# Adding a rank-1 term through ScalarE in PSUM instead of bf16 matmuls, splitting seven Strassen products into two groups, and loading the start-up differently

## Chip, cores, metric

One core of a Trainium2 chip. The metric is device time in microseconds, the median of several executions. All executions quoted here were in the fast state, with a granted TensorE clock of 0.988 to 0.996 (the single run of e4_constant_scale has state unknown and is used for durations only). The time of the kernel before was 2109.68 us (2107.85 to 2117.36, 3 runs).

## The reference

```python
def reference(x, w_in, w_out):            # x [8, 3008, 256], w_in [256, 2048], w_out [2048, 256], fp32
    X = np.fft.fft(np.fft.fft(x, axis=1), axis=2).real     # a 2-D Fourier transform, real part
    X = X.reshape(8 * 3008, 256)
    h = X @ w_in
    g = h * np.cos(h)
    return g @ w_out
```

The kernel uses symmetry. It transforms along the sequence only; the transform along the channels is folded into the first weight matrix. Position k and position -k of the sequence then share their work: with P the even part and Q the odd part, one hidden value is P+Q and its mirror is P-Q. One channel (channel 0) does not fit into the 128 rows of the even matmul and must be added by itself as a rank-1 term: its row over the positions, times its column of weights.

## The kernel before: the parts that matter

The main loop has 376 steps. A step fills one PSUM bank called hp with 512 columns: two blocks of 128 hidden units, side by side, each for 256 positions. Eight steps make a tile (256 positions and their mirrors). The second weight matrix is applied in Strassen's way: seven products of half-size blocks, with sums before and after, instead of eight. In each step the engines do the following. (A limb is one of the three bf16 numbers whose sum stands for one fp32 number.)

```python
def mlp1_even(T, s):                  # TensorE, into the PSUM bank hp
    hp = ppool.tile([128, 512], FP, tag="hp", bufs=2, name="hp")
    for i in range(2):                # P without channel 0, fp32
        matmul(hp[:, i*TW:(i+1)*TW], lhsT=Wc[:, f*128:(f+1)*128], rhs=Rr[:, pos:pos+TW], start=(i == 0), ...)
    for i in range(2):                # channel 0: nine bf16 rows (3 limbs x 3 limbs) stand for one fp32 row
        matmul(hp[:, i*TW:(i+1)*TW], lhsT=Wl[:, f*128:(f+1)*128], rhs=Rl[:, pos:pos+TW], start=False, ...)

def copy_even(T, s):  ...             # ScalarE: pt = -2 * hp            (-2P; TensorE must not go on before)
def mlp1_odd(T, s):   ...             # TensorE: hp += Ws' Ir            (now P+Q)
def copy_plus(T, s):  ...             # ScalarE: h[:, 0:512] = hp
def minus(T, s):      ...             # VectorE: h[:, 512:1024] = pt + hp, reversed   (the subtraction)
# h * cos(h): ScalarE rounds, VectorE takes the remainder, ScalarE sine, VectorE product

def sums(T, s):
    A[5] = A[3] + A[2]; A[4] = A[0] + A[5]              # VectorE
    d = spool.tile([128, 512], FP, tag="d", bufs=DB)
    nc.scalar.copy(out=d, in_=T.h[s][:, 0:512])         # ScalarE
    nc.gpsimd.dma_start(out=d, in_=T.h[s][:, 768:1280], accum_op=ALU.add)   # d += h, by DMA

def mlp2(T, s, between):              # seven Strassen products into four banks, 4 steps behind
    parts = (("Ma",0,B11,A[0]), ("Mb",0,B21,A[1]), ("Mb",1,T2,A[4]), ("Mc",0,T1,A[5]), ("Md",1,T4,A[2]),
             ("Mc",1,T3,d[:,0:256]), ("Md",0,B22,d[:,256:512]))   # mlp1_odd runs ahead of the last two
# ... at the end of a tile: combine(T), four VectorE adds in a row, after the next step's mlp1_even ...
```

The input of each batch but the first is folded (summed and subtracted with its mirror, which shrinks the transform) by 18 VectorE operations, one a step, in steps 10 to 27 of the 47 steps of the batch ahead of it. Four transforms of six fp32 matmuls each follow.

Of the kernel before, what the change touches and what calls it, by code (L numbers as in the profile page):

```python
# [12 lines left out]
BF = mybir.dt.bfloat16  # L13
# [6 lines left out]
ND = 256  # L20
# [9 lines left out]
LAG = 4  # L30
HB = 5
DB = 3
# [47 lines left out]
def _limb_consts():  # L80

    p = np.arange(128)
    i, j = p // 3, p % 3
    return -np.stack([i >= 1, i >= 2, j >= 1, j >= 2], axis=1).astype(np.float32)


@with_exitstack
def kernel(
# [16 lines left out]
    LC_dr = nc.inline_tensor(_limb_consts(), name="limb_masks")  # L105
# [27 lines left out]
    LC = cpool.tile([128, 4], FP, tag="LC")  # L133
    nc.scalar.dma_start(out=LC, in_=LC_dr.ap())

# [53 lines left out]
    w2r = w2.rearrange("p (q e a j) -> p q e a j", e=2, a=4, j=32)  # L189
    wor = moe_w_out.rearrange("(q p) (a e j) -> p q e a j", p=128, e=2, j=32)  # L190
    for e in range(2):
        for a in range(4):
            nc.sync.dma_start(out=w2r[:, :, e, a], in_=wor[:, :, e, a])
# [12 lines left out]

    Rl = cpool.tile([128, RING], BF, tag="Rl")
    Wl = cpool.tile([128, NDFF], BF, tag="Wl")
    nc.vector.memset(Wl, 0.0)
    nc.vector.memset(Rl, 0.0)  # L210
# [7 lines left out]
    r128_dr = dpool.tile([3, NB, HALF], BF, tag="r128", name="r128")  # L218
    wl_dr = dpool.tile([3, NDFF], BF, tag="wl", name="wl")
# [9 lines left out]
    def fold_weights():  # L229
        for q in range(NDFF // 512):  # L230
# [24 lines left out]
            if q % 2:  # L255
                load_row(q // 2)
        with nc.allow_non_contiguous_dma(reason="one row to columns"):
            nc.gpsimd.dma_start(
                out=wex, in_=wx_dr.rearrange("o (f p) -> p (o f)", p=128)
            )  # L260

    def load_row(half):
        cols = slice(half * 1024, (half + 1) * 1024)
        nc.gpsimd.dma_start(out=wx_dr[:, cols], in_=Ws[127:128, cols])
        wf = spool.tile([8, 128], FP, tag="wf", bufs=2, name="wf")
        nc.gpsimd.dma_start(
            out=wf, in_=wx_dr[0, cols].rearrange("(f p) -> f p", p=128)
        )
        state["wf", half] = wf

    def row_to_limbs(half):

        cols = slice(half * 1024, (half + 1) * 1024)
        l3 = spool.tile([8, 3, 128], BF, tag="l3", bufs=2, name="l3")
        split_limbs(state["wf", half], [l3[:, j] for j in range(3)])
        nc.gpsimd.dma_start(
            out=wl_dr[:, cols].rearrange("j (f p) -> f j p", p=128), in_=l3
        )
        for i in range(3):
            nc.gpsimd.dma_start(out=Wl[3 * i : 3 * i + 3, cols], in_=wl_dr[:, cols])  # L280

    def split_limbs(x, limbs):

        for n, limb in enumerate(limbs):
            pin(nc.vector.tensor_copy(out=limb, in_=x))
            if n < 2:
                pin(
                    nc.vector.tensor_tensor(out=x, in0=x, in1=limb, op=ALU.subtract)
                )

    def row_limbs(x, limb, out_, c):

        n = x.shape[0]
        for step in range(3):
            o = out_ if step == 2 else limb
            pin(nc.vector.tensor_copy(out=o, in_=x))
            if step < 2:
                pin(
                    nc.vector.scalar_tensor_tensor(
                        out=x,  # L300
                        in0=limb,
                        scalar=LC[0:n, c + step : c + step + 1],
                        in1=x,
                        op0=ALU.mult,
                        op1=ALU.add,
                    )
                )
# [766 lines left out]
```

## Time and profile before

| | busy, share of the span |
|---|---|
| TensorE (PE) | 97% |
| VectorE (DVE) | 84% |
| ScalarE (ACT) | 68% |
| span of the profiled run | 2105.9 us |

The head of the profile page of the kernel before, and its chain of waits (the work that ended last, followed back from the end):

```profile
span 2105.9 us, 26765 instructions
PE 2050.6 (97%) x9540; PEld 1703.0 (81%) x9540; DVE 1778.3 (84%) x2438; ACT 1428.1 (68%) x1976; POOL 352.3 (17%) x409
...
PE 83%; DVE 11%; DMA 2%; issue 2%; ACT 1%; another core or an unknown queue 1%; SPq 0%; DVEq 0%; POOL 0%; ACTq 0%
```

The chain is TensorE for 83% of the span. The busy share alone would not have told this: the skill's page "Trainium Kernel Development and Optimization" (Performance Expectations) warns that, because matmuls are pipelined, matmul busy time is a bad measure of how close a kernel is to the roofline. What can be read exactly is when matmuls start. One step in TensorE's timeline (start in us, duration, engine, line, operation, tiles; "x4" means four instructions, because the profile records each fp32 matmul twice):

```profile
1001.22 1.03 PE L633 MATMUL hp<-Rr,Wc 128*128 128x256 f32 x4
1002.08 0.38 PE L645 MATMUL hp<-Rl,Wl 128*128 128x256 bf16 x2
1002.30 0.60 PE L767 MATMUL Ma<-h,w_88 128*128 128x256 f32 x2
1002.73 0.59 PE L767 MATMUL Mb<-h,w_88 128*128 128x256 f32 x2
...
1004.03 0.59 PE L767 MATMUL Md<-h,T_119 128*128 128x256 f32 x2
1004.46 1.03 PE L670 MATMUL hp<-Ir,Ws 127*128 127x256 f32 x4
1005.32 0.60 PE L767 MATMUL Mc<-d,T_118 128*128 128x256 f32 x2
1005.76 0.59 PE L767 MATMUL Md<-d,w_88 128*128 128x256 f32 x2
1006.19 0.59 PE L633 MATMUL hp<-Rr,Wc 128*128 128x256 f32 x2
```

The step is 1006.19 - 1001.22 = 4.97 us. The fp32 products stand 0.43 us apart; the two limb matmuls take 1002.30 - 1002.08 = 0.22 us. No idle time is marked: TensorE's stream has no holes here.

The costs of the operations that the change touches, in the groups of instructions of the kernel before (columns: line, engine, operation, tiles, shapes, count | busy us in all, mean ns of one | idle time just before them and its releaser):

```profile
L659 ACT ACTIVATE pt<-hp 128x512 f32<-128x512 f32 x376 | 221.7, 590 | 227.0 <-PE hp L645 223.8
L706 ACT COPY d<-h 128x512 f32<-128x512 f32 x376 | 229.6, 611 | 68.7 <-DVE h L735 67.1
```

And what TensorE waited for between 36 and 160 us, the start-up (columns: us in total, times, longest):

```profile
PE hp L670 <- ACT pt L659: 20.4, 8, 11.7
PE hp L645 <- DMA Wl<-wl: 9.6, 1, 9.6
PE hp L633 <- DVE Rr L406: 2.5, 1, 2.5
```

The 11.7 us wait ends a chain that begins with a 10.8 us wait of VectorE for the single channel's DMA, so the start-up is held by loads twice.

### The profile page before, as it was taken

The page shows a single profiled execution, that of the slowest core. Times are in us where ns is not written, and L with a number is a line of the kernel's source. Part 1 is how long each engine was busy: PE and PEld are TensorE (multiplying, and loading weights), DVE is VectorE, ACT ScalarE, POOL GpSimd, SP SyncE. Part 2 cuts the span into 40 slices and gives each one's busy share as a digit, 9 for nine tenths or more (in the row PEclk, how much of TensorE's full clock was granted, in tenths as well). Part 3 has the DMA queues.
Part 4 walks back from the last instruction along what each step waited for, and adds up shares of the span by engine and source line. Part 5 has one row for each costly group of instructions (what it writes and reads, how often), then busy time and mean ns, then how long its engine had stood idle before and what let it go on. Part 6 is the DMA issues. An engine that isn't in the chain of part 4 may idle for free.

```text
span 2105.9 us, 26765 instructions
## 1 busy us (share of the span) xinstructions
PE 2050.6 (97%) x9540; PEld 1703.0 (81%) x9540; DVE 1778.3 (84%) x2438; ACT 1428.1 (68%) x1976; POOL 352.3 (17%) x409
## 2 busy tenths in 40 slices
PE   7779999999999999999999999999999999999998
PEld 3558888888888888888888878888788888888877
DVE  6489788997889878898789987899788997888867
ACT  2457667776677667776677766777677776777755
POOL 1111111121111111111111111111111111111111
PEclk9989999999999999999999999999999999999999
DMA  9933343343333333334333334333433332333323
GB/s 249 62 61 64 86 88 71 64 90 71 75 74 64 87 84 71 66 61 88 85 74 61 60 88 94 66 64 64 99 81 64 58 74 50 63 64 71 65 51 66
DMA packets 210510, 159.80 MB, mean 76 GB/s; under 512 B 156845, under 2 KB 156886, under 8 KB 209864
## 3 DMA queue, kind: packets, MB, share of 16 engines
q0 software_dynamic: 56880, 111.25, 28.6%
q1 hardware_dynamic: 153352, 46.84, 10.4%
q8 instruction: 75, 1.23, 0.3%
q14 instruction: 59, 0.48, 0.1%
q10 hardware_dynamic: 144, 0.00, 0.0%
HBM read 34.67 MB, written 24.78 MB: 28 GB/s over the span
## 4 chain that ended last, share of the span: by engine, by line
PE 83%; DVE 11%; DMA 2%; issue 2%; ACT 1%; another core or an unknown queue 1%; SPq 0%; DVEq 0%; POOL 0%; ACTq 0%
PE hp L670 14%; PE hp L633 13%; PE Mc L767 13%; PE Md L767 13%; PE Mb L767 13%; PE Ma L767 7%; PE hp L645 3%; PE da L391 3%; PE db L391 3%; DVE h L735 2%; DVE r L721 2%; DVE h L688 1%; DVE X L796 1%; DVE h L703 1%; ACT r L728 1%
## 5 line engine op out<-in xcount | busy, mean ns | idle before, releaser
L707 POOL DMA_DIRECT2D d<-h x376 | 323.8, 861 | 1662.4 <-ACT h L684 419.1
L721 DVE TENSOR_TENSOR r<-h,r 128x1024 f32<-128x1024 f32 x376 | 458.2, 1219 | 91.0 <-ACT r L713 91.0
L728 ACT ACTIVATE r<-r,halfpi 128x1024 f32<-128x1024 f32 x376 | 432.8, 1151 | 137.2 <-DVE r L721 136.5
L735 DVE SCALAR_TENSOR_TENSOR h<-h,r 128x1024 f32<-128x1024 f32 x376 | 458.2, 1219 | 72.8 <-ACT r L728 72.8
L670 PE MATMUL hp<-Ir,Ws 127*128 127x256 f32 x1504 | 393.4, 383 | 24.8 <-ACT pt L659 24.5
L713 ACT ACTIVATE r<-h 128x1024 int32<-128x1024 f32 x376 | 394.8, 1050 | 4.8 <-DVE h L688 3.7
L633 PE MATMUL hp<-Rr,Wc 128*128 128x256 f32 x1504 | 388.9, 381 | 2.5 <-DVE Rr L406 2.5
L659 ACT ACTIVATE pt<-hp 128x512 f32<-128x512 f32 x376 | 221.7, 590 | 227.0 <-PE hp L645 223.8
L684 ACT COPY h<-hp 128x512 f32<-128x512 f32 x376 | 219.9, 585 | 194.5 <-PE hp L670 194.2
L670 PEld LDWEIGHTS hp<-Ir,Ws 127*128 127x128 f32 x1504 | 278.8, 190 | 79.2 <-ACT pt L659 43.3
L688 DVE TENSOR_TENSOR h<-pt,hp 128x512 f32<-128x512 f32 x376 | 257.2, 684 | 88.2 <-ACT h L684 84.9
L633 PEld LDWEIGHTS hp<-Rr,Wc 128*128 128x128 f32 x1504 | 286.6, 191 | 49.0 <-DVE Rr L406 3.1
L706 ACT COPY d<-h 128x512 f32<-128x512 f32 x376 | 229.6, 611 | 68.7 <-DVE h L735 67.1
L767 PE MATMUL Ma<-h,w_88 128*128 128x256 f32 x752 | 225.6, 382 | 0.3 <-ACT X L781 0.3
L767 PE MATMUL Mc<-d,T_118 128*128 128x256 f32 x752 | 225.4, 381 | 0.4 <-DMA d<-h 0.4
L767 PE MATMUL Mb<-h,w_88 128*128 128x256 f32 x752 | 224.7, 380 | 1.0 <-DVE X L796 1.0
L767 PE MATMUL Mc<-h,T_116 128*128 128x256 f32 x752 | 224.4, 380 | 0.4 <-DVE X L796 0.4
L767 PE MATMUL Mb<-h,T_117 128*128 128x256 f32 x752 | 224.6, 380 | 0.0
L767 PE MATMUL Md<-h,T_119 128*128 128x256 f32 x752 | 224.2, 380 | 0.1
L767 PE MATMUL Md<-d,w_88 128*128 128x256 f32 x752 | 224.1, 380 | 0.0
L704 DVE TENSOR_TENSOR h<-h 128x256 f32<-128x256 f32 x376 | 159.8, 425 | 12.9
L703 DVE TENSOR_TENSOR h<-h 128x256 f32<-128x256 f32 x376 | 159.7, 425 | 12.9
(349 smaller groups left out, 1896.2 us busy)
## 6 DMA issues: line engine op xcount, KB each, us to landing
d<-h POOLq DMA_DIRECT2D x376, 256.0 KB, 3.2
out_dram<-tr SPq DMA_DIRECT2D x252, 64.0 KB
h<-in_moe_w_in_dram SPq DMA_DIRECT2D x4, 512.0 KB
w_88<-in_moe_w_out_dram SPq DMA_DIRECT2D x8, 256.0 KB
out_dram<-tr SPq DMA_DIRECT2D x128, 4.0 KB
out_dram<-tr SPq DMA_DIRECT2D x32, 56.0 KB
out_dram<-tr SPq DMA_DIRECT2D x32, 48.0 KB
out_dram<-tr SPq DMA_DIRECT2D x32, 40.0 KB
```

What stands on the lines that cost most here:

```text
L633: nc.tensor.matmul(hp[:, i * TW : (i + 1) * TW], lhsT=Wc[:, f * 128 : (f + 1) * 128], rhs=Rr[:, pos : pos + TW], start=(i == 0), stop=Fals ...
L659: nc.scalar.activation(out=T.pt[s], in_=T.hp[s], func=AF.Copy, bias=0.0, scale=-2.0)
L670: nc.tensor.matmul(T.hp[s][:, i * TW : (i + 1) * TW], lhsT=Ws[0:127, f * 128 : (f + 1) * 128], rhs=Ir[:, pos : pos + TW], start=False, sto ...
L684: pin(nc.scalar.copy(out=T.h[s][:, 0:512], in_=T.hp[s]))
L688: nc.vector.tensor_tensor(out=T.h[s][:, 1023:511:-1], in0=T.pt.pop(s), in1=T.hp.pop(s), op=ALU.add,)
L706: pin(nc.scalar.copy(out=d, in_=T.h[s][:, 0:512]))
L707: pin(nc.gpsimd.dma_start(out=d, in_=T.h[s][:, 768:1280], accum_op=ALU.add))
L713: nc.scalar.activation(out=r[:, 0:n].bitcast(I32), in_=h[:, 0:n], func=AF.Copy, bias=0.25, scale=1.0)
L721: nc.vector.tensor_tensor(out=r[:, 0:n], in0=h[:, 0:n], in1=k, op=ALU.subtract)
L728: nc.scalar.activation(out=r[:, 0:n], in_=r[:, 0:n], func=AF.Sin, bias=halfpi, scale=TWO_PI)
L735: nc.vector.scalar_tensor_tensor(out=h[:, 0:n], in0=h[:, 0:n], scalar=TWO_PI, in1=r[:, 0:n], op0=ALU.mult, op1=ALU.mult,)
L767: nc.tensor.matmul(T.M[bank][:, half * TW : (half + 1) * TW], lhsT=lhsT[:, s], rhs=rhs, start=(s == 0 and n in (0, 1, 3, 4)), stop=(s == 7 ...
```

## The change

The intent is to take the limb matmuls off TensorE. ScalarE writes channel 0 as a product (a row spread over all partitions, times a per-partition scale) into the hp bank, and the even and odd matmuls accumulate on top of it. That this can work at all is in the skill's page "PSUM — Partial Sum Buffer" (The four PSUM rules): ScalarE writes neither set nor clear the hidden written bits, and a matmul without the first-of-group flag adds where the bit is set. Here the start-up's weight-folding matmuls have set those bits in both hp banks and nothing clears them later. To make room on ScalarE the copy into d goes: the seven products are split into a group of three (3 steps behind), after which the DMA may add into h itself, and a group of four (4 steps behind). The end of a tile is split the same way.

```diff
+    def channel_0(T, s):
+        T.hp[s] = ppool.tile([128, 512], FP, tag="hp", bufs=2, name="hp")
+        for i in range(2):
+            nc.scalar.mul(T.hp[s][:, i*TW:(i+1)*TW], Rb[:, pos:pos+TW], wex[:, f:f+1])
 def mlp1_even(T, s):
-        hp = ppool.tile([128, 512], FP, tag="hp", bufs=2, name="hp")
-                    ... start=(i == 0) ...
+                    ... start=False ...
-        for i in range(2):                      # limb matmuls
-            nc.tensor.matmul(hp..., lhsT=Wl[...], rhs=Rl[...], ...)
 def sums(T, s):
-        d = spool.tile([128, 512], FP, tag="d", bufs=DB, name="d")
-        pin(nc.scalar.copy(out=d, in_=T.h[s][:, 0:512]))
-        pin(nc.gpsimd.dma_start(out=d, in_=T.h[s][:, 768:1280], accum_op=ALU.add))
-    def mlp2(...), def combine(T)
+    def products_1(T, s):   # Ma B11 A0; Mb B21 A1; Mb T2 A4; then
+        nc.gpsimd.dma_start(out=h[:, 0:512], in_=h[:, 768:1280], accum_op=ALU.add)
+    def products_2(T, s):   # Mc T1 A5; Md T4 A2; Mc T3 h[0:256]; Md B22 h[256:512]
+    def combine_1(T): ...   # Ma, Mb: one ScalarE copy, one VectorE add
+    def combine_2(T): ...   # Mc, Md: three VectorE adds
 # the loop
+        stage(i + 1, channel_0)                 # right after the rounding
+        stage(i - LAG1, products_1)             # LAG1 = 3
+        if ...: combine_1(...)
+        stage(i, mlp1_odd)
+        stage(i - LAG2, products_2)             # LAG2 = 4
+        stage(i, copy_plus)
+        if ...: combine_2(T)
 # start-up
-    eight loads of w_out in 128-byte pieces straight into w2
+    three loads in 1 KB rows, put into place by six ScalarE copies
-    limb arithmetic of the channel's row and weights;  at(2, load_ext)
+    load_ext() ahead of the loop
     (some other start-up operations move by one or two steps)
```

More of the change, by code (lines that the diff above doesn't have):

```diff
@@ L12 @@
 I32 = mybir.dt.int32
-BF = mybir.dt.bfloat16
 U32 = mybir.dt.uint32
@@ L29 @@
 BW = 3 * NE
-LAG = 4
+LAG1 = 3
+LAG2 = 4
 HB = 5
-DB = 3
 def _dft_consts():
@@ L77, in _row_consts @@
     return np.stack([neg, HALF - 5 - 6 * p, last], axis=1).astype(np.uint32)
-def _limb_consts():
-    p = np.arange(128)
-    i, j = p // 3, p % 3
-    return -np.stack([i >= 1, i >= 2, j >= 1, j >= 2], axis=1).astype(np.float32)
 @with_exitstack
@@ L104 @@
     IX_dr = nc.inline_tensor(_row_consts(), name="row_table")
-    LC_dr = nc.inline_tensor(_limb_consts(), name="limb_masks")
     cpool = ctx.enter_context(tc.tile_pool(name="consts", bufs=1))
@@ L132 @@
     nc.sync.dma_start(out=ix, in_=IX_dr.ap())
-    LC = cpool.tile([128, 4], FP, tag="LC")
-    nc.scalar.dma_start(out=LC, in_=LC_dr.ap())
     def load_x(b):
@@ L187, with place_w2 @@
             MC[ri, kodd] = m
-    w2r = w2.rearrange("p (q e a j) -> p q e a j", e=2, a=4, j=32)
-    wor = moe_w_out.rearrange("(q p) (a e j) -> p q e a j", p=128, e=2, j=32)
-    for e in range(2):
-        for a in range(4):
-            nc.sync.dma_start(out=w2r[:, :, e, a], in_=wor[:, :, e, a])
+    W2_PARTS = ((0, 6), (6, 12), (12, 16))
+    w2_parts = []
+    for f0, f1 in W2_PARTS:
+        st = spool.tile([128, 1536], FP, tag="h", bufs=HB, name="st")
+        nc.sync.dma_start(
+            out=st[:, 0 : (f1 - f0) * ND].rearrange("p (q c) -> p q c", c=ND),
+            in_=moe_w_out[f0 * 128 : f1 * 128, :].rearrange("(q p) c -> p q c", p=128),
+        )
+        w2_parts.append(st)
+    def place_w2(n):
+        f0, f1 = W2_PARTS[n]
+        src = w2_parts[n][:, 0 : (f1 - f0) * ND].rearrange(
+            "p (q a e j) -> p q a e j", a=4, e=2, j=32
+        )
+        dst = w2[:, f0 * ND : f1 * ND].rearrange(
+            "p (q e a j) -> p q e a j", e=2, a=4, j=32
+        )
+        for e in range(2):
+            pin(nc.scalar.copy(out=dst[:, :, e], in_=src[:, :, :, e]))
     halfpi = cpool.tile([128, 1], FP, tag="halfpi")
@@ L205 @@
     Ir = cpool.tile([127, RING], FP, tag="Ir")
-    Rl = cpool.tile([128, RING], BF, tag="Rl")
-    Wl = cpool.tile([128, NDFF], BF, tag="Wl")
-    nc.vector.memset(Wl, 0.0)
-    nc.vector.memset(Rl, 0.0)
+    Rb = cpool.tile([128, RING], FP, tag="Rb")
     T1 = cpool.tile([128, NF // 2, 128], FP, tag="T1")
@@ L217 @@
     Rb4 = cpool.tile([128, NB], FP, tag="Rb4")
-    r128_dr = dpool.tile([3, NB, HALF], BF, tag="r128", name="r128")
-    wl_dr = dpool.tile([3, NDFF], BF, tag="wl", name="wl")
+    r128_dr = dpool.tile([NB, HALF], FP, tag="r128", name="r128")
     wx_dr = dpool.tile([1, NDFF], FP, tag="wx", name="wx")
@@ L255, in fold_weights @@
             if q % 2:
-                load_row(q // 2)
-        with nc.allow_non_contiguous_dma(reason="one row to columns"):
-            nc.gpsimd.dma_start(
-                out=wex, in_=wx_dr.rearrange("o (f p) -> p (o f)", p=128)
-            )
-    def load_row(half):
-        cols = slice(half * 1024, (half + 1) * 1024)
-        nc.gpsimd.dma_start(out=wx_dr[:, cols], in_=Ws[127:128, cols])
-        wf = spool.tile([8, 128], FP, tag="wf", bufs=2, name="wf")
-        nc.gpsimd.dma_start(
-            out=wf, in_=wx_dr[0, cols].rearrange("(f p) -> f p", p=128)
-        )
-        state["wf", half] = wf
-    def row_to_limbs(half):
-        cols = slice(half * 1024, (half + 1) * 1024)
-        l3 = spool.tile([8, 3, 128], BF, tag="l3", bufs=2, name="l3")
-        split_limbs(state["wf", half], [l3[:, j] for j in range(3)])
-        nc.gpsimd.dma_start(
-            out=wl_dr[:, cols].rearrange("j (f p) -> f j p", p=128), in_=l3
-        )
-        for i in range(3):
-            nc.gpsimd.dma_start(out=Wl[3 * i : 3 * i + 3, cols], in_=wl_dr[:, cols])
-    def split_limbs(x, limbs):
-        for n, limb in enumerate(limbs):
-            pin(nc.vector.tensor_copy(out=limb, in_=x))
-            if n < 2:
-                pin(
-                    nc.vector.tensor_tensor(out=x, in0=x, in1=limb, op=ALU.subtract)
-                )
-    def row_limbs(x, limb, out_, c):
-        n = x.shape[0]
-        for step in range(3):
-            o = out_ if step == 2 else limb
-            pin(nc.vector.tensor_copy(out=o, in_=x))
-            if step < 2:
-                pin(
-                    nc.vector.scalar_tensor_tensor(
-                        out=x,
-                        in0=limb,
-                        scalar=LC[0:n, c + step : c + step + 1],
-                        in1=x,
-                        op0=ALU.mult,
-                        op1=ALU.add,
+                cols = slice((q - 1) * 512, (q + 1) * 512)
+                nc.gpsimd.dma_start(out=wx_dr[:, cols], in_=Ws[127:128, cols])
+                with nc.allow_non_contiguous_dma(reason="one row to columns"):
+                    nc.gpsimd.dma_start(
+                        out=wex[:, (q - 1) * 4 : (q + 1) * 4],
+                        in_=wx_dr[:, cols].rearrange("o (f p) -> p (o f)", p=128),
                     )
-                )
     def fold_x(L):
@@ L369, in fold_first @@
         tt(out=g.unsqueeze(2), in0=c[2], in1=c[3], op=ALU.add)
-        e = spool.tile([128, 6, 9], FP, tag="xb", bufs=1, name="xb")
+        e = spool.tile([128, 1536], FP, tag="C", bufs=1, name="xb")[:, 0:768]
+        e = e.rearrange("p (m d) -> p m d", d=128)
         tt(
             out=e,
-            in0=a.unsqueeze(2).to_broadcast([128, 6, 9]),
-            in1=g.unsqueeze(2).to_broadcast([128, 6, 9]),
+            in0=a.unsqueeze(2).to_broadcast([128, 6, 128]),
+            in1=g.unsqueeze(2).to_broadcast([128, 6, 128]),
             op=ALU.add,
@@ L460, in dft_first @@
     def dft_first(xb, **kw):
-        x9 = spool.tile([128, 1536], FP, tag="C", bufs=1, name="x9")[0:9, 0:RUN]
-        lt = spool.tile([128, 1024], BF, tag="ob", bufs=2, name="lt")[0:9, 0:RUN]
-        low, high = ring_writers(x9, 0, 0)
-        def low_limbs(op, a, z):
-            low(op, a, z)
-            row_limbs(x9[:, a:z], lt[:, a:z], Rl[0:9, a:z], 0)
-        def high_limbs(op, a, z):
-            high(op, a, z)
-            row_limbs(x9[:, NE:RUN], lt[:, NE:RUN], Rl[0:9, NE:RUN], 0)
-        return dft_pair(0, 0, xb, 9, low_limbs, high_limbs, None, **kw)
+        low, high = ring_writers(Rb, 0, 0)
+        return dft_pair(0, 0, xb, 128, low, high, None, **kw)
     def dft_I(b, kodd, EO, **kw):
@@ L525, in evacuate @@
                     )
+            nc.sync.dma_start(out=r128_dr, in_=rx[:, 0:HALF])
             nc.sync.dma_start(
@@ L530, in dft_ext @@
         return evacuate
-    def limb_ext(n):
-        rx = X1[:, 0:HALF]
-        limb = X0.bitcast(BF)[:, (n % 2) * 1536 : (n % 2) * 1536 + HALF]
-        pin(nc.vector.tensor_copy(out=limb, in_=rx))
-        if n < 2:
-            pin(nc.vector.tensor_tensor(out=rx, in0=rx, in1=limb, op=ALU.subtract))
-        nc.sync.dma_start(out=r128_dr[n], in_=limb)
     def spread_ext(b, i=0):
@@ L545, in spread_ext @@
             m = min(HALF - i, RING - pos)
-            for n in range(3):
-                nc.sync.dma_start(
-                    out=Rl[3 * n : 3 * n + 3, pos : pos + m],
-                    in_=r128_dr[n, b : b + 1, i : i + m].to_broadcast([3, m]),
-                )
+            nc.sync.dma_start(
+                out=Rb[:, pos : pos + m],
+                in_=r128_dr[b : b + 1, i : i + m].to_broadcast([128, m]),
+            )
             i += m
@@ L624 @@
         pass
+    def channel_0(T, s):
+        pos = (T.q * TW) % RING
+        T.hp[s] = ppool.tile([128, 512], FP, tag="hp", bufs=2, name="hp")
+        for i in range(2):
+            f = 2 * s + i
+            pin(
+                nc.scalar.mul(
+                    T.hp[s][:, i * TW : (i + 1) * TW],
+                    Rb[:, pos : pos + TW],
+                    wex[:, f : f + 1],
+                )
+            )
     def mlp1_even(T, s):
         pos = (T.q * TW) % RING
-        hp = ppool.tile([128, 512], FP, tag="hp", bufs=2, name="hp")
         for i in range(2):
@@ L633, in mlp1_even @@
                 nc.tensor.matmul(
-                    hp[:, i * TW : (i + 1) * TW],
+                    T.hp[s][:, i * TW : (i + 1) * TW],
                     lhsT=Wc[:, f * 128 : (f + 1) * 128],
                     rhs=Rr[:, pos : pos + TW],
-                    start=(i == 0),
-                    stop=False,
-                    skip_group_check=True,
-                )
-            )
-        for i in range(2):
-            f = 2 * s + i
-            pin(
-                nc.tensor.matmul(
-                    hp[:, i * TW : (i + 1) * TW],
-                    lhsT=Wl[:, f * 128 : (f + 1) * 128],
-                    rhs=Rl[:, pos : pos + TW],
                     start=False,
@@ L653, in mlp1_even @@
             )
-        T.hp[s] = hp
     def copy_even(T, s):
@@ L704, in sums @@
         pin(nc.vector.tensor_tensor(out=A[4], in0=A[0], in1=A[5], op=ALU.add))
-        d = spool.tile([128, 512], FP, tag="d", bufs=DB, name="d")
-        pin(nc.scalar.copy(out=d, in_=T.h[s][:, 0:512]))
-        pin(nc.gpsimd.dma_start(out=d, in_=T.h[s][:, 768:1280], accum_op=ALU.add))
-        T.d[s] = d
     def act_round(h, r, n):
@@ L743, in act_product @@
         )
-    def mlp2(T, s, between=None):
-        if s == 0:
-            T.M = {
-                n: ppool.tile([128, 512], FP, tag=n, bufs=1, name=n)
-                for n in ("Ma", "Mb", "Mc", "Md")
-            }
-        h, d = T.h.pop(s), T.d.pop(s)
-        A = [h[:, i * TW : (i + 1) * TW] for i in range(6)]
-        parts = (
-            ("Ma", 0, B11, A[0]),
-            ("Mb", 0, B21, A[1]),
-            ("Mb", 1, T2, A[4]),
-            ("Mc", 0, T1, A[5]),
-            ("Md", 1, T4, A[2]),
-            ("Mc", 1, T3, d[:, 0:256]),
-            ("Md", 0, B22, d[:, 256:512]),
-        )
-        for n, (bank, half, lhsT, rhs) in enumerate(parts):
-            if n == 5 and between is not None:
-                between()
-            pin(
-                nc.tensor.matmul(
-                    T.M[bank][:, half * TW : (half + 1) * TW],
-                    lhsT=lhsT[:, s],
-                    rhs=rhs,
-                    start=(s == 0 and n in (0, 1, 3, 4)),
-                    stop=(s == 7),
-                    skip_group_check=True,
-                )
-            )
@@ L777, in combine, with product @@
-    def combine(T):
-        X = spool.tile([128, 1536], FP, tag="C", bufs=1, name="X")
-        pin(nc.scalar.copy(out=X[:, 1280:1536], in_=T.M["Ma"][:, 0:TW]))
-        def blocks(t):
-            return t.rearrange("p (i c) -> p i c", c=TW)
-        def twice(i):
-            return X[:, i * TW : (i + 1) * TW].unsqueeze(1).to_broadcast([128, 2, TW])
-        Xb = blocks(X)
-        for o, a, b in (
-            (Xb[:, 0:5:4], twice(5), blocks(T.M["Mb"])),
-            (Xb[:, 1:3], twice(4), blocks(T.M["Mc"])),
-            (Xb[:, 3], Xb[:, 2], T.M["Mc"][:, 0:TW]),
-            (Xb[:, 1:3], Xb[:, 1:3], blocks(T.M["Md"])),
-        ):
-            pin(nc.vector.tensor_tensor(out=o, in0=a, in1=b, op=ALU.add))
-        T.X = X
+    def product(T, s, bank, half, lhsT, rhs, first):
+        if bank not in T.M:
+            T.M[bank] = ppool.tile([128, 512], FP, tag=bank, bufs=1, name=bank)
+        pin(
+            nc.tensor.matmul(
+                T.M[bank][:, half * TW : (half + 1) * TW],
+                lhsT=lhsT[:, s],
+                rhs=T.h[s][:, rhs * TW : (rhs + 1) * TW],
+                start=(s == 0 and first),
+                stop=(s == 7),
+                skip_group_check=True,
+            )
+        )
@@ new lines, in products_1 @@
+    def products_1(T, s):
+        product(T, s, "Ma", 0, B11, 0, True)
+        product(T, s, "Mb", 0, B21, 1, True)
+        product(T, s, "Mb", 1, T2, 4, False)
+        h = T.h[s]
+        pin(nc.gpsimd.dma_start(out=h[:, 0:512], in_=h[:, 768:1280], accum_op=ALU.add))
+    def products_2(T, s):
+        product(T, s, "Mc", 0, T1, 5, True)
+        product(T, s, "Md", 1, T4, 2, True)
+        product(T, s, "Mc", 1, T3, 0, False)
+        product(T, s, "Md", 0, B22, 1, False)
+        T.h.pop(s)
@@ new lines, in combine_1, with combine_2 @@
+    def combine_1(T):
+        T.X = spool.tile([128, 1536], FP, tag="C", bufs=1, name="X")
+        pin(nc.scalar.copy(out=T.X[:, 1280:1536], in_=T.M["Ma"][:, 0:TW]))
+        add_blocks(T, (0, 5, 4), 5, "Mb")
+    def combine_2(T):
+        add_blocks(T, (1, 3, 1), 4, "Mc")
+        X = T.X
+        pin(
+            nc.vector.tensor_tensor(
+                out=X[:, 768:1024], in0=X[:, 512:768], in1=T.M["Mc"][:, 0:TW], op=ALU.add
+            )
+        )
+        add_blocks(T, (1, 3, 1), None, "Md")
@@ L799, in turn, with add_blocks @@
+    def add_blocks(T, to, twice, bank):
+        X = T.X.rearrange("p (i c) -> p i c", c=TW)
+        o = X[:, to[0] : to[1] : to[2]]
+        a = o if twice is None else X[:, twice : twice + 1].to_broadcast([128, 2, TW])
+        b = T.M[bank].rearrange("p (i c) -> p i c", c=TW)
+        pin(nc.vector.tensor_tensor(out=o, in0=a, in1=b, op=ALU.add))
     def turn(T, sg):
@@ L929 @@
         ops[key]()
-    row_to_limbs(0)
     done_x = dft_first(xb, banks=("Ma", "Mb"))
@@ L940 @@
         ops[key]()
+    load_ext()
     side = {}
@@ L960, in start_batch @@
         state["EO"], state["ops"] = fold_x(load_x(b))
-    at(1, lambda: row_to_limbs(1))
+    for n in range(3):
+        at(n // 2, lambda n=n: place_w2(n))
     for n in range(4):
-        at((1, 2, 3, 3)[n], lambda n=n: sum_weights(n))
-    at_dft(2, lambda: dft_R(0, 1, EO))
-    at_dft(5, lambda: dft_I(0, 1, EO))
-    at(2, load_ext)
+        at(2 + n // 2, lambda n=n: sum_weights((0, 1, 2, 3)[n]))
+    at_dft(1, lambda: dft_R(0, 1, EO))
+    at_dft(3, lambda: dft_I(0, 1, EO))
     at(8, fold_ext)
-    at_dft(10, dft_ext)
-    for n in range(3):
-        at(12 + n, lambda n=n: limb_ext(n))
-    at(14, lambda: spread_ext(0, RUN))
+    at_dft(11, dft_ext)
+    at(13, lambda: spread_ext(0, RUN))
     for b in range(1, NB):
         s0 = (b - 1) * steps_b
-        at(s0 + (7 if b == 1 else 1), lambda b=b: start_batch(b))
+        at(s0 + (5 if b == 1 else 1), lambda b=b: start_batch(b))
         for i, key in enumerate(FOLDS):
@@ L1001, in tile_of @@
             T.q = q
-            T.h, T.d, T.hp, T.pt, T.r = {}, {}, {}, {}, {}
+            T.h, T.hp, T.pt, T.r, T.M = {}, {}, {}, {}, {}
             tiles[q] = T
@@ L1008, in stage @@
             fn(*tile_of(i))
-    ahead = -1
-    for i in range(total + LAG):
+    stage(0, channel_0)
+    for i in range(total + LAG2):
         stage(i - 1, minus)
@@ L1014 @@
             fn()
-        if ahead < i:
-            stage(i, mlp1_even)
+        stage(i, mlp1_even)
         stage(i - 2, lambda T, s: act_sine(T.r[s], 1024))
-        if ahead < i:
-            stage(i, copy_even)
+        stage(i, copy_even)
         stage(i - 1, rounded)
+        stage(i + 1, channel_0)
         stage(i - 2, lambda T, s: act_product(T.h[s], T.r.pop(s), 1024))
@@ L1023 @@
         stage(i - 1, lambda T, s: act_rest(T.h[s], T.r[s], 1024))
-        j = i - LAG
-        ends = j % 8 == 7
-        if j >= 0:
-            T, s = tile_of(j)
-            mlp2(T, s, None if ends else lambda: stage(i, mlp1_odd))
-            if ends:
-                del tiles[T.q]
-                stage(i + 1, mlp1_even)
-                combine(T)
-                stage(i + 1, copy_even)
-                ahead = i + 1
-                stage(i, mlp1_odd)
-                for sg in range(2):
-                    at(i + 2 + sg, lambda T=T, sg=sg: turn(T, sg))
-        else:
-            stage(i, mlp1_odd)
-        stage(i, copy_plus)
+        stage(i - LAG1, products_1)
+        if i >= LAG1 and (i - LAG1) % 8 == 7 and i - LAG1 < total:
+            combine_1(tiles[(i - LAG1) // 8])
+        stage(i, mlp1_odd)
+        stage(i - LAG2, products_2)
+        stage(i, copy_plus)
+        if i >= LAG2 and (i - LAG2) % 8 == 7:
+            T = tiles.pop((i - LAG2) // 8)
+            combine_2(T)
+            for sg in range(2):
+                at(i + 2 + sg, lambda T=T, sg=sg: turn(T, sg))
     for sg in range(2):
```

## The prediction

> **What bounds it.** TensorE. The page gives PE 97%, DVE 84%, ACT 68%; the chain that ended last is 83% PE. In the timeline the first matmuls of successive steps (376 steps of 512 hidden columns) stand exactly 4.97 us apart in quiet stretches: eleven fp32 products 0.432 us apart (4.76) and two bf16 limb matmuls (0.22). The waits view shows PE held up only about 4 us between 170 and 2040 us. Three places are not PE-bound: the first 39 us; steps 0 to 15 (39 to 160 us, 121 us where about 89 would do), with waits of 9.6 us for the limb weights' DMA and 10.8 us for the single-channel load; and some steps with input folds, spaced 5.24 us, which is VectorE's own work there.
>
> **Removed.** 752 bf16 matmuls: 0.215 us a step, on the critical path, 376 x 0.215 = 81 us. The ScalarE copy into d (0.61). Limb arithmetic on VectorE before the first step (5.5 us) and at steps 12 to 14 (about 6). Output weights come in 1 KB rows instead of 128-byte pieces (some 20 us of all DMA engines), so the 4-byte channel loads land earlier.
>
> **Added.** Two ScalarE multiplies [128x256] into PSUM a step. The like-sized PSUM copy takes 0.372 us; the Trainium skill (ScalarE: Activation LUTs, Step-by-step) says that a PSUM destination is the faster one for ScalarE and that scaling comes free. No trace here shows this form yet; I take 0.37 each, so ScalarE gains 0.74-0.61 = 0.13 us a step: about 3.6 of 4.75. Six weight-placing copies, once (5 us of ScalarE at steps 0, 1).
>
> **Moved.** (a) The even matmuls now wait for ScalarE, which sits behind VectorE's subtraction and the rounding. (b) The odd matmuls come 3 products after the even ones instead of 5 (1.3 us against 2.15), so the -2x copy between them has less slack: I estimate that VectorE may run about 1 us late before PE stalls. (c) The accumulating DMA starts only after the first product group; it then has about 6.4 us until its result is needed, against 3.7 to 5 us from issue to use in the drain. (d) The first group runs a step earlier.
>
> **Balance.** PE step 4.755. VectorE, from start-to-start times: 3.75 a step, 33.4 a tile of 8 steps (4.17 a step), plus 0.87 per fold: over a batch's 18 fold steps 89 us against 85.6 for PE. So VectorE overtakes PE there: stalls of about 4 us a batch, against 2 now, and possibly a few tenths per tile at the four-block recombination. I charge 20 us in all. Start-up gains about 23 beyond the limbs. The drain, where a DMA now separates the two groups, loses 3.
>
> 2110 - 81 - 23 + 20 + 3 = 2029 us. Range 1998 to 2060. Chances: faster by over 2% 0.90, within 2% 0.08, slower 0.02.
>
> **What would show it.** Quiet steps 4.75 us apart; PE still 96 to 97% busy; step 16 starting near 135 us instead of 160; channel multiplies at 0.35 to 0.42 us; no PE wait for the h DMA in steady state; PE waits for ACT pt (odd matmuls) concentrated in fold steps; ScalarE near 72%, VectorE near 86%.
>
> **What would make it wrong.** Channel multiplies nearer 0.6 us: then quiet steps are 5 us again. The DMA landing over 6 us when output stores queue. VectorE lateness costing several us a tile instead of a batch.

## The result, and the profile after

The changed kernel took 2040.5 us (2037.61 to 2046.8, 4 runs) against 2110.24 us (4 runs of the kernel before in the same rounds), a ratio of 0.9668 with a 95% interval of 0.9635 to 0.9701. Ratios here are the mean time of one kernel's fast runs over that of the other's in the same rounds, so not quite the ratio of the medians. Later it took 2041.46 us, ratio 0.9675 (0.9646 to 0.9704); that was chip 7. The outputs are right.

The same parts of the page for the changed kernel:

```profile
span 2037.6 us, 25884 instructions
PE 1974.4 (97%) x8788; PEld 1662.3 (82%) x8788; DVE 1756.9 (86%) x2411; ACT 1540.8 (76%) x2358; POOL 340.0 (17%) x400
...
PE 61%; DVE 22%; ACT 10%; issue 4%; DMA 2%; SPq 0%; DVEq 0%; POOLq 0%; ACTq 0%
```

TensorE is still 97% busy, but its share of the chain fell from 83% to 61%, and VectorE's doubled: other engines now hold TensorE up in places. One quiet step of its timeline:

```profile
531.38 1.03 PE L583 MATMUL hp<-Rr,Wc 128*128 128x256 f32 x4
532.25 0.60 PE L683 MATMUL Ma<-h,w_86 128*128 128x256 f32 x2
532.68 0.59 PE L683 MATMUL Mb<-h,w_86 128*128 128x256 f32 x2
533.11 0.59 PE L683 MATMUL Mb<-h,T_110 128*128 128x256 f32 x2
533.54 1.03 PE L607 MATMUL hp<-Ir,Ws 127*128 127x256 f32 x4
534.41 0.60 PE L683 MATMUL Mc<-h,T_109 128*128 128x256 f32 x2
...
535.70 0.59 PE L683 MATMUL Md<-h,w_86 128*128 128x256 f32 x2
536.13 0.60 PE L583 MATMUL hp<-Rr,Wc 128*128 128x256 f32 x2
```

The step is 536.13 - 531.38 = 4.75 us. The groups that answer to those shown before, and TensorE's waits in the start-up (36 to 150 us):

```profile
L596 ACT ACTIVATE pt<-hp 128x512 f32<-128x512 f32 x376 | 221.9, 590 | 229.4 <-PE hp L583 226.9
L570 ACT ACTIVATE hp<-Rb,wex 128x256 f32<-128x256 f32 x752 | 355.6, 473 | 12.2
```

```profile
PE hp L607 <- ACT pt L596: 10.0, 5, 3.2
PE Mc L683 <- DMA h<-h: 7.6, 2, 4.9
PE hp L583 <- ACT hp L570: 1.0, 2, 0.7
```

A channel multiply takes 0.473 us. The start-up has a new wait, for the in-place DMA sum.

To say where the time went I take the start of the first even matmul of each step from the trace. Over steps 16 to 360, "excess" is the time between those starts beyond 4.97 us (before, h2) or 4.75 us (all others; unrounded 4.972 and 4.752) a step and 3.81 us for each of the 28 transforms in that stretch. (3.81 is what an undisturbed transform adds, 8.78 - 4.97.)

| trace | step 16 starts | steps 16 to 360 | excess: fold steps + others | step 360 to the end |
|---|---|---|---|---|
| before | 160.0 | 1831.3 | 13.3 + 0.9 | 114.6 |
| after | 141.4 | 1785.1 | 32.2 + 11.6 | 111.1 |
| after, later | 149.9 | 1784.7 | 32.2 + 11.1 | 111.1 |

So of the 68.3 us between the two spans: 376 steps x 0.22 = 82.7 us came from the limb matmuls, about 15 us from the start-up beyond its share of that (160.0 - 141.4 - 16 x 0.22), nothing from the end, and 43.8 - 14.2 = 29.6 us were given back as new stalls. The second trace shows that the run-to-run spread of the changed kernel lies in the start-up: 8.5 us there, under 1 us in the rest. (For it I had expected step 16 at 138 to 146 us; it came at 149.9.)

The waits view shows less than the excess (24.4 us for the odd matmuls waiting for the -2x copy between 142 and 1960 us), because a matmul's recorded end lies later than the moment at which the next could have started (recorded 0.59 us, next start after 0.43). Starts are the safer measure.

Where do the stalls come from? Outside the fold steps 28 tiles end in that stretch. In 18 of them one step takes 5.15 us instead of 4.75; in three, near a transform, it loses 1.3 to 1.4 us; in the other seven, just behind a transform, nothing. VectorE in a stretch with a 5.15 us step:

```profile
540.66 0.69 DVE L730 TENSOR_TENSOR X<-X,Mc 128x512 f32<-128x512 f32 x1 [0.65 <-PE Mc L683]
541.38 0.42 DVE L718 TENSOR_TENSOR X<-X,Mc 128x256 f32<-128x256 f32 x1
541.91 0.69 DVE L730 TENSOR_TENSOR X<-X,Md 128x512 f32<-128x512 f32 x1
542.51 0.68 DVE L625 TENSOR_TENSOR h<-pt,hp 128x512 f32<-128x512 f32 x1
543.11 1.22 DVE L668 SCALAR_TENSOR_TENSOR h<-h,r 128x1024 f32<-128x1024 f32 x1
544.36 0.43 DVE L640 TENSOR_TENSOR h<-h 128x256 f32<-128x256 f32 x1
544.82 0.42 DVE L641 TENSOR_TENSOR h<-h 128x256 f32<-128x256 f32 x1
545.17 1.22 DVE L654 TENSOR_TENSOR r<-h,r 128x1024 f32<-128x1024 f32 x1
```

and what follows in the same timeline on ScalarE and TensorE:

```profile
546.42 1.15 ACT L661 ACTIVATE r<-r,halfpi 128x1024 f32<-128x1024 f32 x1 [0.74 <-DVE r L654]
...
547.37 0.59 PE L683 MATMUL Mb<-h,T_110 128*128 128x256 f32 x2
547.47 0.58 ACT L596 ACTIVATE pt<-hp 128x512 f32<-128x512 f32 x1
...
548.10 1.13 PE L607 MATMUL hp<-Ir,Ws 127*128 127x256 f32 x4
```

VectorE first waits for TensorE's last Mc product, then does the second recombination, and only then the subtraction (L625) of the current step. All that follows is late: product, sums, remainder (L654), then ScalarE's sine, and behind it in ScalarE's order the -2x copy (L596). The odd matmuls (L607) start 0.73 us after the last product instead of 0.43. Three things could be blamed: (A) the place of the recombination in VectorE's order, (B) the short distance from even to odd matmuls, (C) the long channel multiplies on ScalarE.

### The profile page after: what moved, and what is told of

The parts are those of the page before. It is cut to its first block, busy times and chain, and to the rows that moved or that the text cites. A ratio compares the mean times of both kernels' runs of the same rounds, so it can differ in the third digit from the quotient of the medians.

```text
span 2037.6 us, 25884 instructions
## 1 busy us (share of the span) xinstructions
PE 1974.4 (97%) x8788; PEld 1662.3 (82%) x8788; DVE 1756.9 (86%) x2411; ACT 1540.8 (76%) x2358; POOL 340.0 (17%) x400
## 4 chain that ended last, share of the span: by engine, by line
PE 61%; DVE 22%; ACT 10%; issue 4%; DMA 2%; SPq 0%; DVEq 0%; POOLq 0%; ACTq 0%
PE hp L607 11%; PE Mc L683 10%; PE Md L683 10%; PE hp L583 9%; PE Mb L683 9%; DVE r L654 7%; PE Ma L683 5%; DVE h L668 5%; ACT r L661 4%; PE db L348 3%; DVE h L625 3%; PE da L348 3%; ACT r L646 2%; DVE X L730 2%; DVE h L640 2%
## 5 line engine op out<-in xcount | busy, mean ns | idle before, releaser
L698 POOL DMA_DIRECT2D h<-h x376 | 318.2, 846 | 1603.8 <-PE Mb L683 556.6
L654 DVE TENSOR_TENSOR r<-h,r 128x1024 f32<-128x1024 f32 x376 | 458.6, 1220 | 117.3 <-ACT r L646 117.0
L607 PE MATMUL hp<-Ir,Ws 127*128 127x256 f32 x1504 | 395.3, 385 | 37.1 <-ACT pt L596 34.4
L596 ACT ACTIVATE pt<-hp 128x512 f32<-128x512 f32 x376 | 221.9, 590 | 229.4 <-PE hp L583 226.9
L570 ACT ACTIVATE hp<-Rb,wex 128x256 f32<-128x256 f32 x752 | 355.6, 473 | 12.2
L607 PEld LDWEIGHTS hp<-Ir,Ws 127*128 127x128 f32 x1504 | 280.5, 190 | 101.5 <-ACT pt L596 65.7
L625 DVE TENSOR_TENSOR h<-pt,hp 128x512 f32<-128x512 f32 x376 | 256.3, 682 | 12.9 <-ACT h L621 12.6
L683 PE MATMUL Mc<-h,T_111 128*128 128x256 f32 x752 | 225.2, 381 | 8.5 <-DMA h<-h 8.5
L683 PE MATMUL Mc<-h,T_109 128*128 128x256 f32 x752 | 225.2, 380 | 0.0
L683 PE MATMUL Md<-h,w_86 128*128 128x256 f32 x752 | 225.1, 381 | 0.0
L683 PE MATMUL Md<-h,T_112 128*128 128x256 f32 x752 | 223.9, 379 | 0.0
```

The source lines that it names most:

```text
L570: nc.scalar.mul(T.hp[s][:, i * TW : (i + 1) * TW], Rb[:, pos : pos + TW], wex[:, f : f + 1],)
L596: nc.scalar.activation(out=T.pt[s], in_=T.hp[s], func=AF.Copy, bias=0.0, scale=-2.0)
L607: nc.tensor.matmul(T.hp[s][:, i * TW : (i + 1) * TW], lhsT=Ws[0:127, f * 128 : (f + 1) * 128], rhs=Ir[:, pos : pos + TW], start=False, sto ...
L625: nc.vector.tensor_tensor(out=T.h[s][:, 1023:511:-1], in0=T.pt.pop(s), in1=T.hp.pop(s), op=ALU.add,)
L654: nc.vector.tensor_tensor(out=r[:, 0:n], in0=h[:, 0:n], in1=k, op=ALU.subtract)
L683: nc.tensor.matmul(T.M[bank][:, half * TW : (half + 1) * TW], lhsT=lhsT[:, s], rhs=T.h[s][:, rhs * TW : (rhs + 1) * TW], start=(s == 0 and ...
```

## Experiments

Every run is the changed kernel with the edit shown, unless it says otherwise. They were made on different chips, each with its own runs of the kernel before: 2110.93 us (e1, e3, h1, h2; chip 14), 2106.98 us (e2, e5, s1, s2; chip 10) and 2109.18 us (e6, t1, e4 and the repeat of the changed kernel; chip 7). Compare ratios, not times, across calls.

### e1_combine_late: theory A

```diff
-            combine_2(T)
+            if i + 1 < total + LAG2: at(i + 1, lambda T=T: combine_2(T))   # behind the next subtraction
+            else: combine_2(T)
```

> The changed kernel with one edit: the second recombination (three VectorE adds) is recorded one step later, behind the subtraction of that step instead of ahead of it. Theory A (the 0.40 us stall in every tile, and most of the 44 us of extra step time, come from the subtraction standing behind a recombination that itself waits for TensorE's last product): the 5.15 us steps become 4.75, the excess over quiet steps between steps 16 and 360 falls from 44 to under 20 us, the time to about 2012 to 2020. Theory B (odd matmuls too close behind the even ones) and theory C (the channel multiplies at 0.47 instead of 0.37 us load ScalarE): nearly no effect, one step of each tile still 5.15, 2036 to 2042.

Measured: 2031.07 us (2024.44 to 2031.94), ratio 0.9609 (0.9581 to 0.9636). Excess 30.4 in fold steps + 2.8 elsewhere. The 0.40 us stalls are gone from all 18 tiles (what is left of the 11.6 us stands near transforms), so the order on VectorE is one way to remove them. But theory A had claimed most of the 44 us: the fold steps did not move (32.2 to 30.4). It is right for the tile stall and wrong for the rest.

### e3_odd_late: theory B

```diff
 products_2: T1, T4,
+            mlp1_odd of the current step,
             T3, B22
-        stage(i, mlp1_odd)        # was ahead of products_2
```

> The changed kernel with the odd matmuls moved behind two products of the second group, so five products stand between even and odd as in the kernel before. Theory B: the copy in between gets 0.86 us more, the 0.40 us stalls vanish, excess from 44 to about 15 to 25 us, time 2015 to 2025. Theory A: the lateness starts before that copy and the subtraction now also starts 0.86 us later, so the loop subtraction, rounding, multiply, even has no slack left: stalls stay or move to the even matmuls, which would then wait for the channel multiplies; time 2035 to 2060.

Measured: 2022.11 us (2020.91 to 2024.04), ratio 0.9577 (0.9555 to 0.9600). Excess 29.1 + 1.5. This too removes the tile stall, and the feared shortage between subtraction and even matmuls did not come: TensorE's only wait in the main stretch is 6.2 us for the -2x copy. So A and B are two sides of one account, lateness against slack: 0.40 us vanish by making VectorE less late or by granting the copy 0.86 us more. Again the fold steps keep 29 us. The time fell by more than the 13 us of excess; its trace also reached step 16 at 138.7 us, within the spread of the start-up.

### e2_one_multiply: theory C (wrong result on purpose)

```diff
-        for i in range(2): nc.scalar.mul(hp[:, i*TW:(i+1)*TW], Rb[:, pos:pos+TW], wex[:, f:f+1])
+        nc.scalar.mul(hp as [128, 2, 256], Rb[...] broadcast to [128, 2, 256], wex[:, 2*s : 2*s+1])
```

> Wrong result on purpose: the two channel multiplies of a step become one of twice the width with one scale column, about 0.3 to 0.4 us less ScalarE a step. Theory C (the multiplies, 0.47 instead of 0.37 us, are what uses up the slack): the 0.40 us stall per tile vanishes and stalls in fold steps fall, 2018 to 2030. Theory A (the late chain runs subtraction, product, sums, remainder on VectorE, then sine and the -2x copy, and the multiplies are beside it): one step of each tile still 5.1 to 5.2, excess 35 to 44 us, 2032 to 2042.

Measured: 2042.97 us (2042.09 to 2044.7), ratio 0.9701 (0.9677 to 0.9725). ScalarE fell to 71% busy and nothing else changed: excess 32.2 + 11.3. Theory C falls. The trace above says why: the sine waits for VectorE's remainder, and the multiplies are beside that path.

### h1_channel_only and h2_groups_only: the two halves of the change

```diff
 h1: the changed kernel, with mlp2, sums, the tile d, combine, LAG = 4 and the loop of the kernel before,
+        stage(i + 1, channel_0)
```

> Half of the change: channel 0 by ScalarE multiplies and the changed start-up, but the products, the separate tile d with its ScalarE copy, the lag of 4 and the recombination of the kernel before. ScalarE then has 4.4 us of work a step by start-to-start times, of 4.75. If the gain is only the limb matmuls taken from TensorE: quiet steps 4.75, time 2030 to 2045, as the whole change. If the freed copy is needed to make room for the multiplies: quiet steps 4.8 to 5.0 or stalls at every tile end, 2060 to 2115.

Measured: 2044.05 us (2041.4 to 2046.36), ratio 0.9683 (0.9661 to 0.9706). Quiet steps are 4.75 us; excess 36.9 + 9.1.

```diff
 h2: the kernel before (limb matmuls and start-up included), with products_1, products_2, combine_1,
     combine_2, the in-place DMA sum and the loop of the changed kernel, without channel_0
```

> The other half: limb matmuls and the start-up of the kernel before, with the products in two groups and the DMA sum in the h tile. Quiet steps stay 4.97. If the two groups bring nothing by themselves: 2105 to 2125, with small stalls once per tile at the recombination (before had none). If the grouping itself is worth something (ScalarE and VectorE freer): under 2100.

Measured: 2110.4 us (2106.08 to 2116.62), ratio 1.000 (0.9968 to 1.0031). Excess 16.8 + 2.7 at 4.97 us a step.

The gain is therefore the limb matmuls and the start-up; the two groups bring nothing measurable. Their purpose, freeing ScalarE of the copy into d, was met but not needed. The four kernels also make a table of two by two for the loss outside the fold steps: before 0.9 us, h2 (new order, 4.97 us a step) 2.7, h1 (old order, 4.75) 9.1, the changed kernel (new order, 4.75) 11.6. So most of that loss came with the shorter step, which leaves VectorE 0.22 us less, and only about 2 us with the new order (the 4.75 us step also brings the multiplies, which e2 found harmless); theory A names what stands in the way, not what brought the stall out. The heads of the two pages, h1 first, then h2:

```profile
PE 1985.1 (97%) x8788; PEld 1647.1 (81%) x8788; DVE 1762.6 (86%) x2411; ACT 1730.9 (85%) x2734; POOL 341.7 (17%) x400
```

```profile
PE 2054.4 (98%) x9540; PEld 1703.8 (81%) x9540; DVE 1780.8 (85%) x2438; ACT 1260.6 (60%) x1600; POOL 352.4 (17%) x409
```

ScalarE at 85% still keeps up, and at 60% it gains nothing.

### e5_folds_spread: what is left in the fold steps

In fold steps of the changed kernel VectorE is hardly idle: in 101 of the 126, under 0.1 us from one subtraction to the next. From its timeline, one remainder to the next, in a step with a fold and a transpose:

```profile
1128.17 1.22 DVE L654 TENSOR_TENSOR r<-h,r 128x1024 f32<-128x1024 f32 x1
1129.30 0.68 DVE L625 TENSOR_TENSOR h<-pt,hp 128x512 f32<-128x512 f32 x1
1129.90 0.94 DVE L272 TENSOR_TENSOR xl_6291<-xl_6291 128x762 f32<-128x762 f32 x1
1130.76 0.70 DVE L736 STREAM_TRANSPOSE tr<-X 128x512 f32<-128x512 f32 x1
1131.39 1.18 DVE L668 SCALAR_TENSOR_TENSOR h<-h,r 128x1024 f32<-128x1024 f32 x1
1132.61 0.42 DVE L640 TENSOR_TENSOR h<-h 128x256 f32<-128x256 f32 x1
1133.07 0.42 DVE L641 TENSOR_TENSOR h<-h 128x256 f32<-128x256 f32 x1
1133.41 1.22 DVE L654 TENSOR_TENSOR r<-h,r 128x1024 f32<-128x1024 f32 x1
```

1133.41 - 1128.17 = 5.24 us: more than a step of TensorE, before (4.97) and much more so after (4.75). The edit is on top of e3_odd_late:

```diff
-        at(s0 + (5 if b == 1 else 1), start_batch)      # loads the batch's input
-        folds at s0 + 10 + i, one a step
+        at(s0 + (5 if b == 1 else -8), start_batch)
+        folds (b > 1): one a step at steps s0-4 .. s0+27 with i % 8 in (0, 1, 4, 7); the two tiny ones a step later
```

> The run e3_odd_late plus one edit: for batches 2 to 7 the input of a batch is loaded nine steps earlier and its 18 fold operations are spread over 32 steps, only on steps without recombination or transposes, instead of 18 steps in a row. If the 29 us of stalls left in fold steps are VectorE's capacity there (89 us of work in 86 us): they fall to under 10 us (batch 1 is unchanged), time 1998 to 2008. If they come from something else in those steps, such as the input DMA or the accumulating DMA queueing behind it: they stay above 20 us, 2016 to 2024.

Measured: 2015.6 us (2011.43 to 2015.89), ratio 0.9563 (0.9537 to 0.9588), correct. The interval overlaps that of e3 (0.9555 to 0.9600), so it is the step starts that tell the two apart: excess 21.4, of which 15.1 in the old fold steps (29.1 in e3). Half of it went, so the crowding of folds on VectorE is a cause; I expected under 10. The steps show what is left: mostly 0.4 to 0.7 us in the tiles that still carry a fold right after the recombination, and single waits for the in-place DMA sum (3.3 us in two waits). One of these is in step 74, which alone loses 4.7 of the 15.1 us. The input loads moved less than the edit says: in the traces of e3 and e5 they start within a few us of the same place in the loop, ahead of the step at which the code writes them, except two, at 431.2 instead of 437.4 us and at 1396.5 instead of 1414.8. The two waits come right behind these two loads; that the loads cause them was not tested.

### e6_best: all three edits

```diff
 e5 with combine_2 deferred as in e1, and folds at i % 8 in (0, 1, 3, 7)
```

> The three edits that helped, together: second recombination behind the next subtraction, odd matmuls behind two products of the second group, folds of batches 2 to 7 spread over the steps without recombination or transposes. e5 still lost 0.40 us at the step of the first transposes where a fold stood right after the recombination; here a fold never follows it. If lateness of VectorE is the whole cause: excess between steps 16 and 360 under 10 us (21 in e5, 44 in the changed kernel), time 1998 to 2010. If the edits do not add: 2012 to 2018.

Measured: 2017.74 us (2014.37 to 2023.4), ratio 0.9569 (0.9543 to 0.9595). Excess 20.0. The edits do not add. TensorE now waits for the deferred recombination itself to empty Mc (2.3 us in five waits) and for the DMA sum (4.6 us in two). e5 and e6 cannot be told apart by their intervals; both beat the changed kernel and the kernel before, by about 1% and over 4%.

### s1_w2_small_pieces and s2_channel_load_late: the start-up

```diff
 s1: -    three 1 KB-row loads and six ScalarE copies   +    the eight 128-byte-piece loads of the kernel before
 s2: -    load_ext() ahead of the loop                  +    at(2, load_ext)
```

> The changed kernel with the output weights loaded as in the kernel before (128-byte pieces straight into place, no ScalarE placing). If the larger pieces are what shortened the start: step 16 starts at 148 to 158 us instead of about 141, time 2048 to 2055. If removing the limb arithmetic was: step 16 within 4 us of 141, time 2036 to 2044, or a little sooner because six ScalarE copies go.

Measured: 2048.46 us (2044.55 to 2058.93), ratio 0.9722 (0.9698 to 0.9746). The profiled run was its slowest, with step 16 at 159.4 us. Against two kernels that leave the main loop's stalls as they are (e2 at 2042.97, s2 at 2043.46) it is about 5 us slower, but the intervals of the ratios overlap. The larger pieces may be worth something like that; with a start-up that varies by 8 us, it is not shown. In its (slowest) trace TensorE waits 18.0 us for the in-place DMA sum, against 7.6 us in the changed kernel.

> The changed kernel with the 4-byte loads of the single channel issued at step 2, as before, instead of ahead of the loop. If the early issue matters: the fold of the single channel at step 8 waits for them again and step 16 starts 6 to 15 us later, time 2046 to 2055. If not: within 4 us of 141 and 2036 to 2044; the accumulating DMA's wait at step 4 (4.9 us in the changed kernel's trace) may shrink.

Measured: 2043.46 us (2035.38 to 2047.11), ratio 0.9707 (0.9681 to 0.9732), step 16 at 138.7 us. The early issue changed nothing, and the wait for the DMA sum stayed (8.2 us).

### t1_no_small_packets: why the start-up gained less than expected (wrong result on purpose)

```diff
 load_ext:  -   ap=[[SEQ * ND, NB], [ND, 1536], [1, 1]]     # 4-byte pieces
            +   ap=[[SEQ * ND, NB], [1, 1536], [1, 1]]      # 6 KB rows
```

> Wrong result on purpose: the single channel is fetched as 6 KB rows of wrong data instead of 24,576 pieces of 4 bytes; the same bytes, instructions and waits. If these pieces keep the DMA engines full and so cause the start-up's remaining waits (7.6 us of TensorE for the in-place DMA sum among them): that wait falls under 1 us, step 16 starts at 122 to 132 us instead of 138 to 146, time about 10 to 18 us below the changed kernel. If the start-up is bound by its own chain of engines: within 4 us of it.

Measured: 2026.38 us (2025.29 to 2027.81), ratio 0.9612 (0.9581 to 0.9644), 15 us below the changed kernel; step 16 at 127.6 us. TensorE's waits in the start-up:

```profile
PE hp L607 <- ACT pt L596: 10.2, 5, 3.2
PE hp L583 <- ACT hp L570: 1.0, 2, 0.7
```

The 7.6 us wait for the DMA sum is gone, and so is most of the spread between runs. So it is the 4-byte pieces that the in-place sum waits behind in the changed kernel, where 4-byte packets take 68% of the 16 DMA engines' time from 55 to 75 us. In the kernel before they are in the same place: from 50 to 65 us, when the limb weights are awaited, they take 90% of that time. No run took them away there, so for the limb weights it is likely and not shown.

### e4_constant_scale: what makes a multiply 0.47 us (wrong result on purpose)

```diff
-        both halves: nc.scalar.mul(hp half, Rb, wex column)
+        first half: nc.scalar.activation(hp half, Rb, func=Copy, scale=0.5);  second half as before
```

> Wrong result on purpose, one look: the first of the two multiplies has a constant scale, the second keeps its scale column. If the column costs the extra 0.1 us over the 0.37 us of a like-sized copy: first 0.36 to 0.39, second 0.47 to 0.48. If the source (SBUF) or the destination (PSUM) costs it: both 0.46 to 0.48.

Its two groups, constant scale and scale column:

```profile
L568 ACT ACTIVATE hp<-Rb 128x256 f32<-128x256 f32 x376 | 141.6, 377 | 0.0
L575 ACT ACTIVATE hp<-Rb,wex 128x256 f32<-128x256 f32 x376 | 179.7, 478 | 12.2
```

The scale column costs the 0.10 us. The place of the destination does not, and neither does coming second (in the changed kernel, where both have a column, the first takes 0.468 us and the second 0.478). It looks like a cost per instruction and not per element: the one multiply of e2, twice as wide, took 0.681 us with a column, the -2x copy of that width 0.590 with a constant (it reads PSUM, so this is no clean contrast).

## Why the prediction was right, and where it was off

The forecast was 2029 us with a range of 1998 to 2060; measured 2040.5. The mechanism and the sign of every term but the last held. Nothing large cancelled by luck: the two big misses, start-up (8 us in the first trace) and stalls (10 us), both made the kernel slower than forecast; the limbs and the drain gave back 5 us.

- "quiet steps 4.75 us apart": 4.75, and h1 against h2 shows that this is the limb matmuls alone. The term of 81 us measured 82.7.
- "Start-up gains about 23 beyond the limbs": 15 us in the first trace, about 7 in the second. The order of causes was partly right. The limb-weight wait went, but the loads of 4-byte pieces still held the DMA engines and the in-place sum took over as the thing that waits, 7.6 us; "4-byte channel loads land earlier" was of no use (s2). t1 shows the cause.
- "I charge 20 us in all" for stalls: 29.6 us. By the first trace this is the largest mis-sized term (by the second it is the start-up). The fold part (about 4 us a batch against 2) measured 32.2 - 13.3 = 18.9 us, 2.7 us more a batch. The "few tenths per tile" were real: 0.40 us in 18 of 28 tiles, which with the three dearer ones makes 10.7 us more than before outside the fold steps, by the recombination standing ahead of the subtraction (e1) against a copy with little slack (e3). The prediction had named both halves and summed them too low.
- "The drain ... loses 3": it lost nothing (114.6 - 111.1 = 3.5 = 16 x 0.22).
- "channel multiplies at 0.35 to 0.42 us": 0.473, because of the scale column (e4). The prediction took from the skill that scaling comes free; the last section says what else that page has. The longer multiply was named as a danger and was harmless, since the multiplies are not on the late path (e2). ScalarE was 76% busy instead of the 72% forecast.
- "no PE wait for the h DMA in steady state": 0.2 us between 142 and 1960 us.
- The intent's second half, room on ScalarE, was not questioned in the prediction and turned out to be neutral (h1, h2).

Left open: the last 20 us of excess in e5 and e6, of which the DMA-sum waits and the tiles with folds are seen but not removed, and how the 7 to 15 us of start-up gain divide between limb arithmetic and load size.

## What to carry to other kernels

When one engine is full in every quiet step, an operation taken off it is worth its start-to-start time times the count (here 81 us forecast, 82.7 measured); the loss comes from the busy phases, where the next engine (here VectorE, 86% busy) now sets the pace, so add up each engine's work per phase and not per span. A stall of a few tenths per period is lateness exceeding slack: it can be removed at either end, by moving late work behind what heads the chain or by giving the waiting engine other work first, and doing both brought no more here (e6). Before freeing an engine, ask whether its time is on the path at all: here a ScalarE copy of 0.6 us a step (h2 against before) and 0.26 us of the multiplies (e2) could be taken away without any effect.

## What the Trainium skill lacked or had wrong

- "ScalarE: Activation LUTs" (Step-by-step) calls the affine scale free, as an immediate or a per-partition column. Here the column costs 0.10 us of an instruction of 128x256: 0.478 against 0.377 us with a constant. The page isn't wrong throughout: a later section of it (What ACT_TABLE_LOAD costs) gives about 93 ns for each per-partition pointer operand, which agrees with this 0.10 us. Who reads only the first section, as the prediction did, is misled.
- The same page says that ScalarE writes to PSUM faster than to SBUF. Here a constant-scale instruction from SBUF to PSUM took 0.377 us, a copy of the same shape from PSUM to SBUF 0.365 us (the recombination's copy of Ma in the changed kernel, its median). No advantage shows; source and operation differ too, so it isn't a clean contrast.
- "DMA: Bandwidth & Descriptors" (Anatomy of one DMA) gives 2.0 us plus bytes over 436 GB/s; for the 256 KB sum that is an estimate of 2.6 us. The profile's median from issue to landing was 3.3 us for this accumulating SBUF-to-SBUF transfer, and in the start-up the first one took 10.4 us from issue (60.26 us) to the matmul that waited for it (70.63 us), behind 4-byte pieces. The formula says nothing of either.
- "Trainium Kernel Development and Optimization" (Performance Expectations) offers weight-load busy share, beside the arithmetic share of peak, as a good measure of how close a kernel is to the roofline. Here it was 81%, 82% and 82% for kernels of 2110, 2040 and 2016 us: as flat as the matmul share that it is to replace, so it doesn't tell these kernels apart. Start-to-start times of matmuls did.
